# Halving the chunk pairs from the first one on, with the first pair's B and C loaded in blocks: a Mamba-2 scan feeding a PReLU feed-forward layer

## The chip, the cores and the metric

The kernel runs on one core of a Trainium2 chip. The metric is the device time of one execution, in microseconds (us). A core has five engines with queues of their own: TensorE (PE, matrix products), VectorE (DVE), ScalarE (ACT), GpSimd (POOL) and SyncE (SP), which here only issues loads and stores. They meet through semaphores. Sixteen DMA engines move the data.

## The reference

Four batches, eight heads, 768 tokens, head width D = 32, state width N = 16. The first half is a scan over chunks; its output, turned to tokens by features (3072 x 256), goes through a feed-forward layer of width 2048.

```python
for c in range(nc):                          # in chunks
    cum = np.cumsum(log_a, axis=-1)
    L = np.exp(cum[..., :, None] - cum[..., None, :]) * causal
    M = np.einsum('bhin,bhjn->bhij', Cc, Bc) * L
    y_intra = np.einsum('bhij,bhjd->bhid', M, xc)
    y_inter = np.einsum('bhin,bhnd->bhid', Cc, state) * np.exp(cum)[..., None]
    y[:, :, sl] = y_intra + y_inter
    state = decay_full * state + sum_j(B_j x_j decay_from_j)

h = x @ w_in                                 # x: (3072, 256), w_in: (256, 2048)
g = np.maximum(h, 0.0) + alpha * np.minimum(h, 0.0)
return g @ w_out                             # w_out: (2048, 256)
```

x, a, B and C come as float32, the feed-forward weights and alpha in double width; the kernel makes float32 of them.

## The kernel before

The scan works in chunks of Q = 128 tokens, two chunks k = 0, 1 to a pair, twelve pairs `gp`, three to a batch. Four chunks (two pairs) are a group of GT = 512 tokens; the feed-forward layer takes a group at a time.

A pair has these steps. Loads: B and C (`nat`), x (`xt`), the running products of a (`ap`, also called `pf`), and the decays a of each head copied to all partitions (`abc`). B and C are turned so that the state index lies on the partitions (`bc`), either by four transposes on PE (L640, in the opening L807) or by one on VectorE, from loads in blocks of 8 tokens (`turn_bc`, L545). The decays become a triangular matrix for each head by a scan on VectorE (`scan_half`, L532 and L538; in the opening L855 and L908) whose second operand is an identity: `dec`. C is split into even and odd heads (`cz`, L650/L813, ACT) and multiplied by the running product (`cd`, L653/L957, POOL). The gram products C B^T (PE; L713, L702, in the opening L822) are multiplied by `dec` (L724, in the opening L851). `added` (L600, L589, in the opening L831) is what the pair adds to the state: B times its decay to the end (`bn`, L476, POOL) times x. `states` (L613) adds it up on VectorE and POOL masks it (`sm`, L616). Last, the output y is the sum of state products (L768, L750; in the opening L870) and x products (L776, L758; in the opening L878), and ACT copies it to `xT`.

The pairs have two layouts. Pairs 0 to 5 (`gp < HALF`) hold a chunk on all 128 partitions: a head's decay matrix is 128 x 128, so both chunks and eight heads take 2048 columns, of which the upper triangle's blocks are partly zero. Pairs 6 to 11 hold the tokens of chunk k on half k of the partitions, as two sub-blocks j of HQ = 64 tokens. A head then takes only SQ = 192 columns (128 for the first 64 source tokens, 64 for the others), and PE works on tiles of 32 x 64 (gram) or 64 x 32 (the others), the two chunks side by side. The terms that come from the state and cross from one half to the other need copies of `cd` and the masked state moved to the other half of the partitions (`shifted`: L661 on ACT, L663 on POOL).

The stages. `first_two` does pairs 0 and 1 by hand (the opening), and in between the first feed-forward products for the first 256 tokens (`hidden_two`, L1011, called with f = 0 and 2), as soon as the weights of piece 0 are converted. Its loads come from `load_pair(0)`, `load_rows` and `load_a` (decays of a, L133 and L126), `load_pair(1)` and `load_second` (L223). The weights come in 16 pieces of 512 KB (`load_weights`, L249), converted in four steps (`convert_a`, `sign`, `convert_b`, `convert`; L265 to L318). `keep_warm` (L326) issues matmuls on constants whose results aren't used: 8 at the start, 6 before the first gram, 2 before the first x products. Then group 0 is finished with `hidden` (L996, one feature block f on 512 tokens) and `output` (L1034), while pairs 2 and 3, in large pieces, stand in the gaps, and pair 4 begins. From there on five more groups run with fewer products, on sums of blocks of weights and x (L1095 and L1120), and pairs 4 to 11 (`fine`) go in small pieces between them. There `added` of pair gp + 1 stands behind the x products of pair gp, in what is left of the same PSUM tiles (`beside`).

The order on every engine is written out by hand, and each engine works in that order. A DMA issue takes time on the queue that issues it, and SP issues nearly all of them, in the order of the program: in the opening a, al_n, B and C of pair 0 (L188), x (L192), the first two weight pieces, the copy-out of the decays (`rows_out`, L441: z are the decays, pf the products), B, C and x of pair 1, two pieces, pair 2. There are eight DMA semaphores in turn, so an issue also waits for the one eight before it to land.

Of the kernel before, what the change touches and what calls it, by code (L numbers as in the profile page):

```python
# [9 lines left out]
F32 = mybir.dt.float32  # L10
# [12 lines left out]
def kernel(  # L23
# [47 lines left out]
    WARM = 8  # L71
# [8 lines left out]
    HALF = NP // 2  # L80
# [9 lines left out]
    lda = ctx.enter_context(tc.tile_pool(name="lda", bufs=3))  # L90
# [48 lines left out]
    def load_tokens(dst, src, t0):  # L139


        d = dst.rearrange("p j (h w) -> p j h w", h=H)
        for k in range(2):
            for j in range(2):
                t = t0 + k * Q + j * HQ
                nc.sync.dma_start(out=d[HQ * k : HQ * (k + 1), j],
                                  in_=src[:, t : t + HQ, :].rearrange("h p w -> p h w"))

    def load_spread(gp, b, c):

        for w, t in enumerate(loads["p", gp][1] if gp >= HALF else ()):
            rows = scratch["z", b // 2].rearrange("(b h c) t -> b c h t", b=2, h=H)
            for k in range(2):
                nc.sync.dma_start(
                    out=t[HQ * k : HQ * (k + 1), : 4 * SQ].rearrange("p (h t) -> p h t", h=4),
                    in_=rows[b % 2, c + k, 4 * w : 4 * w + 4].unsqueeze(0)
                    .to_broadcast([HQ, 4, SQ]))
        for k, t in enumerate(loads["p", gp][1] if gp < HALF else ()):
            rows = scratch["z", b // 2].rearrange("(b h c) t -> b c h t", b=2, h=H)[b % 2, c + k]
            nc.sync.dma_start(out=t.rearrange("p (h t) -> p h t", h=H),  # L160
                              in_=rows.unsqueeze(0).to_broadcast([P, H, Q]))

    def load_pair(gp, decays=True):


        b, c = divmod(2 * gp, CPB)
        turned = gp > GC
        nat = ldx.tile([P, 3, 2, H * N], F32, name="nat")
        xt = ldx.tile([P, 2, HD], F32, name="xt")

        ap = ldx.tile([P, 2 * Q], F32, name="ap")
        if gp == 0:
            load_a(ap, b, c)
        elif gp >= NB:
            rows = scratch["pf", b // 2].rearrange("(b h c) t -> b h (c t)", b=2, h=H)
            rows = rows[b % 2, :, c * Q : (c + 2) * Q]
            nc.sync.dma_start(out=ap, in_=rows.unsqueeze(1).to_broadcast([H, N, 2 * Q]))
        if gp == 0:
            load_rows(0, nc.scalar)
            nc.sync.dma_start(out=al_n, in_=moe_alpha.rearrange("(k p) -> k p", p=P))  # L180
        abc = []
        later = []
        if gp >= HALF:
            load_tokens(nat[:, 0], B[b], c * Q)
        for k in range(2 if gp < HALF else 0):
            ts = slice((c + k) * Q, (c + k + 1) * Q)
            for i, src in enumerate((B,) if turned else (B, C)):
                nc.sync.dma_start(out=nat[:, i, k].rearrange("p (h n) -> p h n", h=H),  # L188
                                  in_=src[b, :, ts, :].rearrange("h p n -> p h n"))

            def load_x(k=k, ts=ts):
                nc.sync.dma_start(out=xt[:, k].rearrange("p (h d) -> p h d", h=H),  # L192
                                  in_=x[b, :, ts, :].rearrange("h p d -> p h d"))

            if gp < NB:
                later.append(load_x)
            else:
                load_x()
        for load_x in later:
            load_x()  # L200
        if gp == 0:
            loads["a", 1] = prep.tile([P, 2 * Q], F32, name="a1")
            load_a(loads["a", 1], b, c + 2)
        for i, src in enumerate((B, C) if turned else ()):


            for e in range(2):
                first = src[b, e : e + 1, c * Q : (c + 2) * Q, :]
                nc.sync.dma_start(out=nat[:, 1 + e, i],
                                  in_=bass.AP(tensor=first.tensor, offset=first.offset,  # L210
                                              ap=[[2 * S * N, P // 32], [8 * N, 32], [1, 8 * N]]))
        for k in range(2 if gp >= NB else 0):
            abc.append(lda.tile([P, H * Q], F32, name="abc"))
        loads["p", gp] = nat, abc, xt, ap
        if gp >= HALF:
            load_tokens(xt, x[b], c * Q)
        if decays:
            load_spread(gp, b, c)

    def load_second():  # L220

        rows = scratch["pf", 0].rearrange("(b h c) t -> b h (c t)", b=2, h=H)
        nc.sync.dma_start(out=loads["p", 1][3], in_=rows[0, :, 2 * Q : 4 * Q].unsqueeze(1)  # L223
                          .to_broadcast([H, N, 2 * Q]))

    al_n = const.tile([NF, P], F32, name="al_n")
    load_pair(0)
# [95 lines left out]
    def keep_warm(to, n, cols=2 * Q):  # L323

        for i in range(n):
# [6 lines left out]
    ident_h = const.tile([P, H * Q], F32, name="ident_h")  # L332
    nc.vector.tensor_copy(out=ident_h.rearrange("p (h t) -> p h t", h=H),
                          in_=ident.unsqueeze(1).to_broadcast([P, H, Q]))
# [12 lines left out]
    nc.gpsimd.tensor_tensor(out=hmask, in0=hmask, in1=bmask[:, P:], op=ALU.add)  # L347
    zeros = const.tile([P, Q], F32, name="zeros")
    nc.gpsimd.memset(zeros, 0.0)
# [46 lines left out]
    def halve_identity():  # L396

        for s in range(2):
            nc.scalar.copy(
                out=ident_p[0][HQ:].rearrange("p (a s t) -> p s a t", a=2, s=2)[:, s],  # L400
                in_=ident[HQ:, HQ * (1 - s) : HQ * (2 - s)].unsqueeze(1).to_broadcast([HQ, 2, HQ]))

    def rows_swapped():

        prs = prep.tile([RW, Q], F32, name="rpf")
        for h in range(2):
            nc.scalar.copy(out=prs[:, HQ * h : HQ * (h + 1)],
                           in_=held["pr"][:, HQ * (1 - h) : HQ * (2 - h)])
        held["prs"] = prs

    def rows_clamp(i):
        rows = loads.pop(("r", i))
        d0 = prep.tile([RW, SQ], F32, name="r0")
        nc.vector.tensor_scalar(out=d0[:, :Q], in0=rows, scalar1=1e-6, scalar2=1.0,
                                op0=ALU.max, op1=ALU.min)
        if i:
            nc.vector.tensor_scalar(out=d0[:, Q + 1 :], in0=rows[:, HQ + 1 :], scalar1=1e-6,
                                    scalar2=1.0, op0=ALU.max, op1=ALU.min)
        held[i] = d0

# [10 lines left out]
    def rows_out(i):  # L431


        d0 = held.pop(i)[:, : SQ if i else Q]
        rpf = prep.tile([RW, Q], F32, name="rpf")
        nc.vector.tensor_tensor_scan(out=rpf, data0=d0[:, :Q], data1=zeros[:RW], initial=1.0,
# [6 lines left out]
    def rows_turn(i, pr):  # L443
# [8 lines left out]
        if i == 0:  # L452
            nc.scalar.copy(out=t, in_=ps[:, :RW])
# [7 lines left out]
        if i == 0:  # L461
            nc.scalar.copy(out=alpha, in_=ps[:, RW : RW + NF])
# [978 lines left out]
```

## Time and profile before

| what | us |
|---|---|
| median of three runs | 359.79 (358.23 to 360.84) |
| profiled execution, its own time | 359.9 |
| span of its instructions | 358.2 |
| PE busy | 350.5 (98%), 2878 matmuls |
| PE weight loads busy | 288.3 (80%) |
| VectorE busy | 239.9 (67%) |
| ScalarE busy | 173.8 (49%) |
| GpSimd busy | 205.4 (57%) |
| first `hidden` (L996) starts | 28.69 |
| granted TensorE clock | 0.999 |

The page gives the busy time of each engine, then the span in forty slices (about 9 us each; a digit is the busy share in tenths), then the DMA queues and the chain of work that ended last. The other views used are windows (busy time of each engine and count of instructions, clock, DMA share and GB/s between two times), the chain cut to a window, and groups of instructions by line and shape. "SPq" is the issuing queue of SP.

### The profile page before, as it was taken

How to read it: one execution, taken by the hardware profiler on the slowest of the kernel's cores; microseconds unless marked ns; L12 is line 12 of the kernel's file. 1: busy time of each engine (PE TensorE's matmuls, PEld its weight loads, DVE VectorE, ACT ScalarE, POOL GpSimd, SP SyncE). 2: the span in 40 equal slices, each digit the busy share in tenths (PEclk: the TensorE clock that was granted, in tenths of full speed). 3: DMA queues.
4: the chain of work that ended last, by engine and by line, in shares of the span. 5: the costliest groups of instructions: out<-in, count | busy, mean ns of one | idle time of the engine just before them, and what ended most of it. 6: DMA issues, size and time to landing. Idle time of an engine off the chain costs nothing.

```text
span 358.2 us, 7528 instructions
## 1 busy us (share of the span) xinstructions
PE 350.5 (98%) x2878; PEld 288.3 (80%) x2878; DVE 239.9 (67%) x466; ACT 173.8 (49%) x386; POOL 205.4 (57%) x222
## 2 busy tenths in 40 slices
PE   8899999999999999999999999999999999999994
PEld 8676665578788788888888888888888888888883
DVE  6987986998748756857647847757847533654272
ACT  3577666535356346346246345345445343444330
POOL 4876568589939755725655725646726544632521
PEclk9999999999999999999999999999999999999999
DMA  6989999608255403403513413413001002002003
GB/s 110 182 186 303 326 198 258 140 17 176 88 98 118 94 2 76 102 2 88 92 30 85 79 48 79 89 41 73 1 4 29 0 2 31 0 2 30 0 15 77
DMA packets 105453, 30.19 MB, mean 84 GB/s; under 512 B 79864, under 2 KB 101320, under 8 KB 105416
## 3 DMA queue, kind: packets, MB, share of 16 engines
q1 hardware_dynamic: 104488, 29.45, 37.2%
q8 instruction: 23, 0.38, 0.5%
q10 hardware_dynamic: 928, 0.25, 0.3%
q14 instruction: 14, 0.11, 0.1%
HBM read 26.32 MB, written 3.37 MB: 83 GB/s over the span
## 4 chain that ended last, share of the span: by engine, by line
PE 92%; SPq 3%; DMA 1%; DVE 1%; issue 1%; ACT 1%; POOLq 0%
PE bank L1095 34%; PE hp L1120 28%; PE bank L1034 8%; PE hp L996 6%; PE ss L1120 6%; SPq L188 2%; PE hp L1011 2%; PE ss L758 1%; PE ss L702 1%; DMA nat<-in_C_dram 1%; PE ss L750 1%; PE ss L776 1%; PE ss L713 1%; PE ss L589 1%; PE ss L768 0%
## 5 line engine op out<-in xcount | busy, mean ns | idle before, releaser
L1177 POOL TENSOR_TENSOR gt<-gt 128x512 f32<-128x512 f32 x58 | 74.1, 1277 | 21.1 <-DVE gt L1105 16.3
L1095 PE MATMUL bank<-gt,w_out 128*128 128x256 f32 x320 | 83.5, 381 | 0.0
L1095 PEld LDWEIGHTS bank<-gt,w_out 128*128 128x128 f32 x320 | 60.1, 190 | 9.2 <-issue 1.0
L1105 DVE SCALAR_TENSOR_TENSOR gt<-hp,s_mul,gt 128x256 f32<-128x256 f32 x96 | 42.0, 479 | 29.0 <-ACT gt L1103 26.8
L1167 POOL TENSOR_TENSOR gt<-gt 128x512 f32<-128x512 f32 x20 | 25.4, 1269 | 62.6 <-DVE gt L1105 57.2
L1095 PE MATMUL bank<-gt,ws 128*128 128x256 f32 x240 | 59.5, 379 | 0.0
L1103 ACT ACTIVATE gt<-hp,s_alpha 128x256 f32<-128x256 f32 x96 | 40.3, 471 | 34.5 <-PE hp L1120 31.4
L1095 PEld LDWEIGHTS bank<-gt,ws 128*128 128x128 f32 x240 | 45.6, 190 | 6.2
L1120 PE MATMUL hp<-xs,w_in 128*128 128x256 f32 x160 | 41.9, 384 | 0.0
L1120 PE MATMUL hp<-xs,ws 128*128 128x256 f32 x160 | 41.1, 380 | 0.0
L1146 DVE TENSOR_TENSOR hp<-hp,u 128x512 f32<-128x512 f32 x20 | 14.0, 699 | 35.8 <-ACT u L1144 35.8
L1120 PEld LDWEIGHTS hp<-xs,ws 128*128 128x128 f32 x160 | 30.3, 190 | 4.3 <-POOL xs L1075 0.2
L1120 PEld LDWEIGHTS hp<-xs,w_in 128*128 128x128 f32 x160 | 29.7, 190 | 4.5
L1034 PE MATMUL bank<-w_out,gt 128*128 128x256 f32 x128 | 31.0, 384 | 0.0
L1034 PEld LDWEIGHTS bank<-w_out,gt 128*128 128x128 f32 x128 | 23.6, 190 | 6.5 <-issue 3.1
L1120 PE MATMUL ss<-xT,w_in 128*128 128x256 f32 x96 | 24.6, 379 | 0.0
L996 PE MATMUL hp<-xT,w_in 128*128 128x512 f32 x48 | 22.7, 596 | 0.2 <-DVE gt L1023 0.2
L616 POOL TENSOR_TENSOR sm<-state,bmask 128x256 f32<-128x256 f32 (+1 forms) x10 | 6.2, 617 | 29.0 <-DVE state L613 29.0
L532 DVE TENSOR_TENSOR_SCAN dec<-abc,bank 128x192 f32<-128x192 f32 x48 | 22.6, 522 | 0.0
L1135 ACT COPY m<-hp 128x512 f32<-128x512 f32 x8 | 4.7, 586 | 35.7 <-PE hp L1120 35.7
L1144 ACT COPY u<-hp 128x512 f32<-128x512 f32 x20 | 11.7, 585 | 19.4 <-PE hp L1120 19.4
L1105 DVE SCALAR_TENSOR_TENSOR gt<-c,s_mul,gt 128x256 f32<-128x256 f32 x40 | 20.6, 555 | 0.0
(201 smaller groups left out, 609.6 us busy)
## 6 DMA issues: line engine op xcount, KB each, us to landing
abc<-z SPq DMA_DIRECT2D x24, 192.0 KB
raw<-in_moe_w_in_dram SPq DMA_DIRECT2D x8, 512.0 KB
raw<-in_moe_w_out_dram SPq DMA_DIRECT2D x8, 512.0 KB
abc<-z SPq DMA_DIRECT2D x8, 512.0 KB
out_dram<-o_sb SPq DMA_DIRECT2D x32, 64.0 KB
nat<-in_B_dram SPq DMA_DIRECT2D x26, 64.0 KB
nat<-in_C_dram SPq DMA_DIRECT2D x24, 64.0 KB
xt<-in_x_dram SPq DMA_DIRECT2D x12, 128.0 KB
```

Source lines behind the costliest of these rows:

```text
L188: nc.sync.dma_start(out=nat[:, i, k].rearrange("p (h n) -> p h n", h=H), in_=src[b, :, ts, :].rearrange("h p n -> p h n"))
L532: nc.vector.tensor_tensor_scan(out=dv[:, o : o + SQ], data0=abc[k][:, s : s + SQ], data1=ident_p[0][:, :SQ], initial=0.0, op0=ALU.mult, op ...
L996: nc.tensor.matmul(hp, w_in[:, k, f * P : (f + 1) * P], xts[g][:, k], start=(k == 0), stop=(k == KC - 1))
L1034: nc.tensor.matmul(pos[0][t // 2][:, t % 2], gt[:, t * Q : (t + 1) * Q], w_out[:, f], start=(f == 0 and t % 2 == 0), stop=(f == NF - 1), s ...
L1095: nc.tensor.matmul(ms[g][i][:, h], w, blocks[g, z][n][:, p], start=(q == 0 and h == 0), stop=(q == NQ - 1), skip_group_check=True)
L1103: nc.scalar.mul(o[:, p], h[:, p], s_alpha[:, fs[p]])
L1105: nc.vector.scalar_tensor_tensor(out=o[:, p], in0=h[:, p], scalar=s_mul[:, fs[p]], in1=o[:, p], op0=ALU.mult, op1=ALU.max)
L1120: nc.tensor.matmul(to[:, p], w(2 * z + p), b, start=start and p == 0, stop=True, skip_group_check=True)
L1144: nc.scalar.copy(out=u2, in_=A)
L1146: nc.vector.tensor_tensor(out=Y, in0=Y, in1=u2, op=ALU.add)
L1167: nc.gpsimd.tensor_tensor(out=tc_, in0=g22, in1=g12, op=ALU.subtract)
L1177: eng.tensor_tensor(out=o, in0=x0, in1=x1, op=ALU.subtract)
```

## The change

All pairs take the halved layout: the constant HALF and every branch on it go. `rows_turn` turns the decays to the end on PE into the halved order for both halves of the batches; the identity that the scans use is made in the halved form at the start, so `halve_identity` and `rows_swapped` go. The scans and products of pairs 0 to 5 take the narrower shapes. For pairs 2 and 3, `added` no longer has a slot of its own: it stands behind the gram, in the columns that the narrower gram leaves free (`dps_of`).

In the opening, B and C of pair 0 come as blocks of 8 tokens, C's issued by SP and B's by ACT's queue, right after a; VectorE turns them (`turn_blocks`) ahead of its scans. B in token order for `bn` is issued by ACT, x by SP, the second half of it behind the copy-out of the decays. The decays of pair 1 are no longer computed from a second load of a, but read back from the copied-out rows (`load_heads` into `z1`), and its spread on PE has the same form as that of pair 0. al_n is loaded later and turned behind that spread. The first weight piece is still issued ahead of `first_two`, the second now just ahead of pair 1, whose C is loaded ahead of its B. The warm-ups at the start become 6 and the other two groups go. `abc` is one tile for a pair, two buffers deep, in place of two tiles three deep.

The core of the diff, first the loads:

```diff
-    WARM = 8
+    WARM = 6
...
-    HALF = NP // 2
...
-    lda = ctx.enter_context(tc.tile_pool(name="lda", bufs=3))
+    lda = ctx.enter_context(tc.tile_pool(name="lda", bufs=2))
...
+    def load_blocks(nat, i, src, t0, es=(0, 1), eng=nc.sync):
+        for e in es:
+            first = src[e : e + 1, t0 : t0 + 2 * Q, :]
+            eng.dma_start(out=nat[:, 1 + e, i],
+                          in_=bass.AP(tensor=first.tensor, offset=first.offset,
+                                      ap=[[2 * S * N, P // 32], [8 * N, 32], [1, 8 * N]]))
...
+    def load_heads(dst, key, b, c):
+        rows = scratch[key, b // 2].rearrange("(b h c) t -> b h c t", b=2, h=H)
+        rows = rows[b % 2, :, c : c + 2].rearrange("h c t -> h (c t)")
+        nc.sync.dma_start(out=dst, in_=rows.unsqueeze(1).to_broadcast([H, N, dst.shape[1]]))
...
+    def load_first():
+        nat, _, xt, ap = pair_tiles(0)
+        load_a(ap, 0, 0)
+        load_rows(0, nc.scalar)
+        for e in range(2):
+            load_blocks(nat, 1, C[0], 0, (e,))
+            load_blocks(nat, 0, B[0], 0, (e,), nc.scalar)
+        nc.scalar.copy(out=al_n[:, :1], in_=nc.const_aps.tensor(1.0, [NF, 1], F32))
...
-    load_pair(0)
+    load_first()
...
-    load_next(2)
-    rows_clamp(0)
+    load_next()
+    load_tokens(loads["p", 0][2], x[0], 0, (0,))
+    load_tokens(loads["p", 0][0][:, 0], B[0], 0, eng=nc.scalar)
+    rows_clamp(0, nc.gpsimd)
```

The order of the opening in `first_two` after the change (new lines; what they replace is the function shown above):

```diff
+        sp = spread_rows(z0)
+        pr = rows_scan(0)
+        rows_ends(0, nc.gpsimd)
+        rows_product(0)
+        rows_out(0, ("z",))
+        load_tokens(xt0, x[0], 0, (1,))
+        load_heads(z1.rearrange("p k t -> p (k t)"), "z", 0, 2)
+        rows_out(0, ("pf",))
+        nc.sync.dma_start(out=al_n, in_=moe_alpha.rearrange("(k p) -> k p", p=P))
+        load_next()
+        nat1, _, xt1, pf1 = pair_tiles(1)
+        load_chunks(nat1[:, 1], C[0], 2 * Q)
+        load_tokens(nat1[:, 0], B[0], 2 * Q)
+        load_heads(pf1, "pf", 0, 2)
+        load_tokens(xt1, x[0], 2 * Q)
...
+        bc0 = turn_blocks(nat0)
+        rows_turn(0, pr, spare())
...
+        scans(0, sp, (0,))
...
+        scans(0, sp, (1, 2, 3))
+        gram = [ss(), ss(), spare(), spare()]
+        gram_products(bc0, cz, gram)
+        dps = dps_of(gram)
+        added(dps, bn0, xt0)
...
+        sp = spread_rows(z1)
+        nc.tensor.transpose(sp[0][:, 2 * SQ : 2 * SQ + NF], al_n, ident[:NF, :NF])
+        state_products(y, (None, sm0[0][:, 0]), cd0)
+        x_products(y, xt0, dec[0], (False, True), (1, 0))
...
+        scans(1, sp, (0, 1))
+        bc1 = turn_products(nat1, spare())
...
+        scans(1, sp, (2, 3))
...
+        prelus = [hidden_two(0, 0, 0, spare())]
+        gram = [ss(), ss(), bank(0), bank(1)]
+        gram_products(bc1, cz, gram)
+        dps = dps_of(gram)
+        added(dps, bn1, xt1)
```

And in `pair`, for those that are not `fine` (pairs 2 and 3):

```diff
         else:
-            states(added(ss_tile()))
-            c_decayed()
-            spread_c()
-            decays(0)
-            yield
-            decays(1)
+            products_of_c()
+            scan_heads(dec, abc, 0, 2)
+            yield
+            scan_heads(dec, abc, 2, 2)
+            yield
...
+        gram_products(bc, cz, gram)
+        if not fine:
+            dps = dps_of(gram)
+            added(dps, bn, xt, nk)
+            states(dps)
+            move_states()
```

In `gram_products` and `x_products` the loops are those that the halved pairs had before (L702 and L758), now for all pairs.

## The prediction

> **What bounds the kernel now.** I read the page's busy shares first, then the forty slices, then the chain that ended last, and then one window at a time.
>
> ```profile
> PE 350.5 (98%) x2878; PEld 288.3 (80%) x2878; DVE 239.9 (67%) x466; ACT 173.8 (49%) x386; POOL 205.4 (57%) x222
> ...
> PE   8899999999999999999999999999999999999994
> ...
> PE 92%; SPq 3%; DMA 1%; DVE 1%; issue 1%; ACT 1%; POOLq 0%
> ```
>
> TensorE is busy for 98% of 358.2 us and is 92% of the last chain; only the first two slices are below 9. A window over the middle is plainer: no gap in 310 us.
>
> ```profile
> 30.00:340.00 310.00, 310.00 (x2501) 256.01 (x2500) 205.68 (x402) 153.38 (x342) 181.76 (x184) 1.00 0.35 78
> ```
>
> So from 28.69 us, where the first `hidden` (L996) begins, time is won only by taking work off PE, and what the change takes from DVE or adds to ACT and POOL is covered. In the opening PE waits. The chain over 0 to 31 us, in order of time (start, us, what):
>
> ```profile
> 10.11 2.90 SPq L188
> ...
> 13.06 3.57 DMA nat<-in_C_dram
> 16.63 0.04 issue
> 16.67 0.34 PE hp L807
> 17.04 0.59 ACT bc L810
> ...
> 17.77 1.97 PE hp L1011 x8
> ...
> 24.33 0.38 ACT xT L883
> ...
> 24.76 2.01 PE hp L1011 x8
> ```
>
> The SP queue, which issues the loads, ends the wait until 13 us; then the load of pair 1's C, whose transpose starts at 16.67; then PE and its short feeders until the two `hidden_two` of tokens 256 to 511 start at 24.76. The opening is therefore a matter of when loads land, and only then of arithmetic.
>
> **What the skill says.** "TensorE: Matmul & The Clock Gate", section on packing small matmuls, says that matmuls on different 32x32 tiles of the array run at once. The trace agrees. Pairs 2 to 5 do their gram products with 16 matmuls on four row tiles; pairs 6 and 7, already halved, with 32 on eight tiles, skipping half of the upper block. In this order (start:end, us, PE busy and count):
>
> ```profile
> 41.79:42.86 1.07, 1.07 (x17) 1.00 1.09 349
> 63.05:64.12 1.07, 1.07 (x17) 1.00 0.92 124
> 90.36:91.60 1.24, 1.24 (x17) 1.00 0.67 220
> 118.95:120.03 1.08, 1.08 (x18) 1.00 0.66 108
> 146.59:147.43 0.84, 0.84 (x34) 1.00 0.82 140
> 173.73:174.57 0.84, 0.84 (x34) 1.00 0.29 88
> ```
>
> "TensorEngine Tiling (Array Packing)", Key Properties, says that a change of tiling mode drains the engine. The trace shows about 0.09 to 0.10 us more in the large matmul on either side of each small group. Part 1 of the first page says that the array runs at half rate until about 3.4 us of sustained work, and again after an idle window. Here a 128-column warm-up matmul took 213 ns until 5.95 us and 106 to 112 ns after; no idle stretch in before is long enough to show the second half. "DMA: Bandwidth & Descriptors", on why a DMA increments its semaphore by 16, says that the engines used are the largest number up to 16 that divides the outermost dimension. A block load (L209) has 4 outermost; while such loads ran, the DMA share was 0.26, four engines of sixteen (last columns: clock, share, GB/s):
>
> ```profile
> 101.80:104.20 2.40, 2.40 (x12) 2.09 (x12) 1.66 (x4) 2.03 (x6) 0.35 (x1) 1.00 0.26 74
> ```
>
> **The change part by part: the steady stage.** Pairs 6 to 11 are as before. Pairs 2 to 5 take on their layout. Gram: 1.07 + 1.07 + 1.24 + 1.08 = 4.46 us become 4 x 0.84 = 3.36: -1.1. State and x products (with `added` of the next pair from pair 4 on):
>
> ```profile
> 49.96:51.57 1.61, 1.61 (x65) 1.00 0.94 258
> 71.35:72.74 1.39, 1.39 (x50) 1.00 0.04 12
> 97.84:99.56 1.72, 1.72 (x73) 1.00 0.58 159
> 125.41:127.40 1.99, 1.99 (x98) 1.00 0.04 8
> 152.80:154.54 1.74, 1.74 (x114) 1.00 0.04 9
> 179.94:181.61 1.67, 1.67 (x114) 1.00 0.16 45
> ```
>
> The halved ones of pairs 6 and 7 take 1.74 and 1.67. Pair 5 comes down to 1.74 (-0.25) and pair 4 to 1.66 (-0.06). Pairs 2 and 3 lack `added` (0.23 by itself at pair 4), so I take about 1.42 and 1.19: -0.19 and -0.20. Sum -0.7. Then `added` of pairs 2 and 3 leaves its own slots (L600, 0.25 and 0.36) and stands straight behind the gram: it still costs some 0.25 each, but the two pairs of switches, about 0.19 each, go, and the double-size group at 55.60 shrinks: -0.3. In all -2.1 us; the uncertain terms are pairs 2 and 3 and the switches, so -1.7 to -2.5.
>
> Hidden beside it: per pair, DVE loses 8 x (664 - 522) = 1.1 us of scans and 4 x (680 - 550) = 0.5 of products. ACT gains two copies of C's product at 297 ns, POOL two of the state at 287. The decays of a pair shrink from 1 MB to 0.79 MB, and two whole-pair buffers replace three half-pair ones. If that cover failed PE would show gaps; the same pieces show none in pairs 6 to 11.
>
> **The change part by part: the opening.** Removed on PE: transposes of pair 0 (0.66), the second spread (L511, 32 by 288 ns, overlapped), and warm-ups of 6 and 2. On DVE: scans of 1206 ns over 512 columns become 384 columns; from 522 for 192 and 664 for 256 I estimate 0.95, and eight save 2.0 us. Added on DVE: one transpose of blocks (L545's row, 1113 ns) in front of those scans.
>
> Timing by hand. (1) B's and C's first blocks are four DMAs of 128 packets on four engines, which `ap` uses too; the similar 512 packets at 101.8 took 4.1 us. They land near 7.0 (5.5 if the queues drain as `ap` did at 3.6, 7.8 if the two issuing queues interleave badly). The transpose then ends near 8.1, and DVE, in order, holds its scans behind it, although their PE input is there from about 6. (2) DVE finishes pair 0's scans near 12 and its last product at 13.4; its x products end near 15.5, where before they ended at 15.78. (3) On SP some 17 issues stand before the last load of pair 1, at 0.41 to 0.65 us each. Eight may be outstanding, so three of them also wait for a landing: second half of x for C's block, the copy-out of the decays for B's, the next for weight piece 0 (near 8.9). The last of pair 1's B is issued near 16, where C was issued at 14.5 before, and lands near 17.6; the last of x near 21.0. (4) From there: transposes to 18.0, `hidden_two` 1.9, gram 0.84, `added` waits for x until 21.3, states 0.6, the mask on POOL 0.73, moving it on ACT 0.3, products 1.35 and 0.84 beside it, two copies 0.75, both needed before L906. It starts near 25.9 against 24.76: +1.1 (1.0 to 1.4). (5) If blocks land at 5.5 and no issue waits, DVE bounds instead and L906 starts at 22.3 to 23.5: -1.3 to -2.5. I take the middle of (4) and (5), a wash, and keep both ends.
>
> The warm-ups taken away leave PE idle for 2 to 3.3 us about 13 us in. Bounds: nothing, if the small groups still count as work; at most the 1.95 us of a `hidden_two` run at half rate plus as much of the next, 1.9 to 3.4. I take nothing, as each stretch is below 3.4.
>
> **Sum.** 359.9 (profiled) - 2.1 + 0 = 357.8; the median 359.79 stands 0.1 lower: 357.7. A change of 1%, 3.6 us, is about what a measurement of this kernel can tell.
>
> **Rivals.** A, likeliest: the steady gain, the opening a wash: 357.7, own range 356.3 to 359.1. For it: the two ends of the opening lie about equally far on both sides.
>
> B: pair 1's loads aren't stalled and the blocks land early: -2.1 - 2.5 = 355.2. For it: the chain shows 2.90 + 1.46 us of SP waiting at L188, and removing loads from SP onto ACT's queue shortens just that; DVE has 2.0 us less. Against it: 17 issues at 0.6 are 10 us whatever lands.
>
> C, slower: the SP queue reaches pair 1's x late, PE idles meanwhile and comes to the dense stage at half rate. Price: opening +1.4 (up to +4.3 if one issue waits 2.90 for a weight piece, as at 10.11 before), +1.9 for the cold clock, -2.1: 361.0 to 363.9, say 362.5. It decides once PE idles for more than 3.4 us in one stretch before `hidden_two`. For it: without the warm-ups only small matmuls run between 8 and 17 us. Against: before, the weight pieces pass through the same ring and the stage starts on time.
>
> D: the change does not do in the stage what it says: the gain on PE is eaten by gaps, since `added`, states, mask and the moves of pairs 2 and 3 now all follow the gram. From the gram to the state products there are 7.1 us (42.86 to 49.96) for about 0.25 + 0.6 + 0.73 + 0.57, so I hold it unlikely: 359.8.
>
> **How the numbers follow.** A 0.40, B 0.38, C 0.17, D 0.05. Faster by over 1% (below 356.2): nearly all of B, 0.36, and A's tail, 0.05: 0.41. Slower by over 1% (above 363.4): the upper part of C, 0.08. Within: 0.51. Range: B reaches to 354.0 with the opening at -2.5, the stage at -2.5 and 0.8 for the DVE time not accounted for; C is taken in to 361.6. That leaves out some 0.05 below and 0.12 above.
>
> **What would show it.** Right: gram groups of 0.84 in all of pairs 2 to 5, L600's slots gone, PE without a gap between the first `hidden` and 340 us, DVE near 231 us (239.9, less 4 x 1.6 in the pairs, less 2.0 of scans and 0.6 of products in the opening, plus 1.1). For the opening, the start of the dense stage (28.69 before) tells A (within 1), B (2 or more earlier) and C (2 or more later). The chain would name SP and the x or B load of pair 1 in A, DVE in B. Matmuls of 128 columns at about 213 ns after 8 us would show C's clock. Wrong: small groups of pairs 2 to 5 above 1.0 us, or PE gaps in the stage.

## The result, and the profile after

The changed kernel takes 368.66 us (368.17 to 369.12) against 359.37 for the kernel before: ratio 1.0256, 95% interval 1.0214 to 1.0298. The forecast was 357.7 with a range of 354.0 to 361.6. The profiled execution has a span of 367.1 us, 8.9 more than before. Its page, in the same order:

```profile
PE 349.5 (95%) x3235; PEld 287.7 (78%) x3235; DVE 231.2 (63%) x469; ACT 175.6 (48%) x402; POOL 209.0 (57%) x231
...
PE   5568999999999999999999999999999999999996
...
PE 78%; DMA 6%; DVE 5%; POOL 4%; ACT 2%; SPq 2%; issue 1%; POOLq 0%; DVEq 0%; ACTq 0%
```

PE does 1.0 us less work (349.5 against 350.5) and VectorE 8.7 us less, near the 231 us that the prediction gave. The time is lost in waits: the first four slices fell from 8, 8, 9, 9 to 5, 5, 6, 8, and the chain, 92% PE before, is 78% now. Four points on PE divide the loss (us, the last column worked out):

| | before | after | |
|---|---|---|---|
| first `hidden_two` starts | 17.77 | 23.12 | +5.35 |
| from there to the third (tokens 256 on) | 6.99 | 8.91 | +1.92 |
| first `hidden` (L996, now L891) starts | 28.69 | 35.96 | +7.27 |
| from there to the last products (the stage) | 324.35 | 327.44 | +3.09 |
| from there to the end of the span | 5.2 | 3.7 | -1.5 |

The last products of before, of after and of g3_stage (an experiment below), each from its own trace:

```profile
353.04 0.44 PE L1220 MATMUL turned<-ident,c 128*128 128x128 f32 x2 [0.28 <-DVE c L1246]
...
363.40 0.44 PE L1115 MATMUL turned<-ident,c 128*128 128x128 f32 x2 [0.27 <-DVE c L1141]
...
360.18 0.44 PE L1120 MATMUL turned<-ident,c 128*128 128x128 f32 x2 [0.27 <-DVE c L1146]
```

So the opening lost 7.3 us, where a wash was forecast, and the stage lost 3.1, where 2.1 were to be gained. The last row is no effect of the change. There the outputs only have to be copied out and land: fifteen of the eighteen profiled executions of this document take 3.6 to 3.9 us for it, and three (those of before, d2_sum and h2_order) 5.0 to 5.2. Whoever reads the stage up to the end of the span takes this difference for a gain.

PE's waits in the opening (engine and operation that waited, what it waited for: us in all, times, longest) were six small ones before; L1011 waiting 0.8 for `bc` was the longest but for the start. After:

```profile
PE ss L540 <- POOL cz L728: 4.4, 1, 4.4
PE bank L469 <- DVE dec L546: 1.6, 1, 1.6
PE hp L502 <- issue: 1.5, 1, 1.5
PE hp L502 <- DMA nat<-in_B_dram: 1.4, 1, 1.4
...
```

The gram (L540) and `added` (L519, 0.9 us) of pair 0, the spread (L469) and the transposes (L502) of pair 1 all wait for something. The chain over the first 45 us:

```profile
2.26 4.65 DMA nat<-in_C_dram
...
7.00 4.76 DMA z<-r
...
18.57 3.81 DMA nat<-in_B_dram
...
23.33 2.95 PE hp L906 x8
```

It goes through two landings up to 11.8: the block load of C (SP issues the copy-out of the decays at 7.0, after it), and that copy-out, which the read-back of pair 1's decays (L176) needs. SP's own waits up to 24 us show a third landing beside them, and a longer one, that of weight piece 0:

```profile
SPq L145 <- DMA raw<-in_moe_w_in_dram: 2.7, 1, 2.7
SPq L427 <- DMA nat<-in_C_dram: 1.5, 1, 1.5
...
SPq L176 <- DMA z<-r: 0.4, 1, 0.4
```

From 7.4 to 10.1 SP stands at the second half of x, which it issues until 11.4; only 0.4 us are left to the copy-out alone. Then fifteen issues follow each other up to 22.9, pair 1's last B among them at 18.57, and it lands at 22.39. The `hidden_two` behind it ran partly at half rate (2.95 us against 1.97).

In the stage, the gram groups of pairs 2 to 5, which the prediction put at 0.84 (start:end, elapsed, PE busy and count):

```profile
48.61:50.42 1.81, 1.47 (x33) 1.00 1.02 377
70.53:72.62 2.09, 1.48 (x34) 1.00 0.53 50
...
```

Pairs 2 and 3 stop in the middle; pairs 4 and 5 take 0.98 and 1.17. PE has gaps of 1.86 us in all between 49 and 90 us, where before had none, all but 0.06 of it put down to gt on VectorE (L895), which frees the PSUM tile that comes next. Among the waits of all engines from 36 to 130 us, the longest that before does not have is no PE wait:

```profile
ACT moved_c L635 <- POOL cd L632: 7.0, 4, 3.3
```

The next such wait is VectorE's for the loaded decays, 3.3 us in two stops.

### The profile page after: what moved, and what is told of

The parts are those of the page before. It is cut to its first block, busy times and chain, and to the rows that moved or that the text cites. A ratio compares the mean times of both kernels' runs of the same rounds, so it can differ in the third digit from the quotient of the medians.

```text
span 367.1 us, 8302 instructions
## 1 busy us (share of the span) xinstructions
PE 349.5 (95%) x3235; PEld 287.7 (78%) x3235; DVE 231.2 (63%) x469; ACT 175.6 (48%) x402; POOL 209.0 (57%) x231
## 4 chain that ended last, share of the span: by engine, by line
PE 78%; DMA 6%; DVE 5%; POOL 4%; ACT 2%; SPq 2%; issue 1%; POOLq 0%; DVEq 0%; ACTq 0%
PE bank L990 33%; PE hp L1015 28%; PE ss L1015 5%; DMA raw<-in_moe_w_in_dram 3%; PE bank L929 2%; PE hp L906 2%; PE ss L560 2%; PE ss L540 2%; DMA z<-r 1%; DMA nat<-in_C_dram 1%; PE ss L685 1%; DVE gt L895 1%; POOL w_out L308 1%; DMA nat<-in_B_dram 1%; PE hp L891 1%
## 5 line engine op out<-in xcount | busy, mean ns | idle before, releaser
L484 DVE TENSOR_TENSOR_SCAN dec<-abc,bank 128x192 f32<-128x192 f32 x80 | 37.8, 526 | 3.3 <-DMA abc<-z 3.3
L525 POOL TENSOR_TENSOR sm<-state,bmask 128x256 f32<-128x256 f32 (+1 forms) x13 | 8.1, 620 | 30.7 <-DVE state L598 27.7
L891 PE MATMUL hp<-xT,w_in 128*128 128x512 f32 x48 | 22.7, 596 | 0.6 <-DVE gt L895 0.4
L1015 PE MATMUL hp<-xT,ws 128*128 128x256 f32 x80 | 20.5, 379 | 0.0
```

What stands on the lines that cost most here:

```text
L484: nc.vector.tensor_tensor_scan(out=dec[:, h], data0=abc[:, h * SQ : (h + 1) * SQ], data1=ident_p[0][:, :SQ], initial=0.0, op0=ALU.mult, op ...
L525: nc.gpsimd.tensor_tensor(out=sm.rearrange("p k (g m) -> p k g m", g=2), in0=new[:, ks].unsqueeze(2).to_broadcast([P, n, 2, 2 * D]), in1=h ...
L891: nc.tensor.matmul(hp, w_in[:, k, f * P : (f + 1) * P], xts[g][:, k], start=(k == 0), stop=(k == KC - 1))
L1015: nc.tensor.matmul(to[:, p], w(2 * z + p), b, start=start and p == 0, stop=True, skip_group_check=True)
```

## The experiments

All were compared with the kernel before on the same chip. "Start" is where the first `hidden` begins in the one profiled execution, "stage" the time from there to the last products, "rest" from there to the end of the span, with the landing of the outputs in it.

| kernel | ratio (95%) | start | stage | rest |
|---|---|---|---|---|
| before | 1 | 28.69 | 324.4 | 329.5 |
| after | 1.0256 (1.0214 to 1.0298) | 35.96 | 327.4 | 331.1 |
| b1_stage | 1.0100 (1.0071 to 1.0129) | 29.1 | 329.2 | 333.0 |
| c1_later | 1.0050 (1.0033 to 1.0067) | 28.9 | 325.6 | 329.2 |
| c4_abc | 1.0204 (1.0171 to 1.0238) | 29.0 | 332.9 | 336.6 |
| c6_xlater | 1.0035 (1.0021 to 1.0049) | 28.8 | 326.2 | 330.0 |
| g3_stage | 1.0203 (1.0170 to 1.0237) | 36.5 | 323.7 | 327.4 |
| a1_warm | 1.0259 (1.0215 to 1.0304) | 35.8 | 329.3 | 333.2 |
| a2_z1 | 1.0252 (1.0212 to 1.0291) | 36.5 | 327.6 | 331.4 |
| a3_first | 1.0261 (1.0219 to 1.0303) | 37.8 | 325.8 | 329.6 |
| d1_noblock | 1.0214 (1.0187 to 1.0242) | 34.6 | 327.6 | 331.2 |
| d2_sum | 1.0176 (1.0144 to 1.0207) | 34.1 | 327.1 | 332.2 |
| e1_order | 1.0209 (1.0194 to 1.0224) | 36.8 | 325.9 | 329.5 |
| e2_tail | 1.0218 (1.0191 to 1.0246) | 33.5 | 326.1 | 329.7 |
| g1_waits | 1.0200 (1.0166 to 1.0234) | 33.5 | 327.3 | 331.0 |
| g2_all | 1.0139 (1.0097 to 1.0182) | 32.5 | 328.5 | 332.1 |
| h1_best | 1.0127 (1.0094 to 1.0160) | 33.8 | 324.0 | 327.7 |
| h2_order | 1.0049 (1.0027 to 1.0070) | 29.9 | 327.6 | 332.6 |

A start is good to some 2.4 us only: e1_order and e2_tail have the same opening up to the first `hidden_two` and begin it at 22.24 and 19.83 in their profiled executions. These are single executions and need not be typical. Those of e1_order and g2_all are the longest of their runs, 2.2 and 2.8 us above the median, and that of e2_tail is the shortest.

**The stage by itself.** b1_stage takes the opening of before and the halved pairs from 2 on.

```diff
-        load_first(), first_two() of after
+        load_pair(0), load_pair(1), first_two() of before (128 partitions)
...
     identity_bank()
+    halve_identity()
+    rows_turn(0, held['pr'], ss_tile())      # pairs 2 to 5: halved order
     bns[2] = pair_loads(2)
```

> The kernel after, but with the opening of before: its loads, their order, its warm-ups, pairs 0 and 1 on 128 partitions. Only pairs 2 to 5 are halved; the decays to the end of batches 0 and 1 are turned once more (eight small matmuls, about 0.7 us with the switches). If the opening alone made the change slow: the first L891 starts within 0.6 us of 28.7, no gap over 0.1 us in the stage up to 90 us, and the time is 359.4 - 2.1 + 0.7 = 358.0. If the halved pairs themselves make the waits that the trace after shows between 49 and 90 us (gaps of 1.85 us, gram groups of 1.81 and 2.08 us): these show here too, and the time is about 361.

It is slower than before by 1.0%. The second answer came true, and beyond its number: the opening is back at 29.1, and the gaps are there (3.25 us), with gram groups of 1.95 and 2.11. The stage takes 329.2 us against 324.4. So the halved pairs lose time by themselves, even where the opening is that of before. ScalarE, 38 to 43 us (start, us, operation, idle before it), then GpSimd at the same time:

```profile
38.27 0.91 ACT L677 ACTIVATE cz<-bc,par 128x256 f32<-128x256 f32 x2
40.53 0.62 ACT L681 COPY moved_c<-cd 64x128 f32<-64x128 f32 x2 [1.35 <-POOL cd L678]
41.57 0.67 ACT L265 ACTIVATE wt<-raw 128x512 f32<-128x512 f32 x1 [0.42 <-DMA raw<-in_moe_w_in_dram]
```

```profile
38.55 1.27 POOL L318 TENSOR_TENSOR w_out<-wr,wg 128x512 uint32<-128x512 uint32 x1 [0.88 <-DVE wr L296]
39.77 0.73 POOL L678 TENSOR_TENSOR cd<-bc,ap 128x256 f32<-128x256 f32 x1
42.40 0.82 POOL L267 TENSOR_SCALAR wt<-wt 128x512 f32<-128x512 f32 x1 [1.90 <-ACT wt L265]
```

The two copies take 0.6 us. But `cd`, which they copy, stands on GpSimd behind a weight conversion that waits for VectorE, so ScalarE stands still for 1.35 us, the next weight's first step comes later, GpSimd waits 1.90 for that, and VectorE and PE are next. Over 28 to 92 us it is 5.1 us of such waits in three stops.

c1_later moves only these copies (pairs 2 and 3), behind the gram:

```diff
         def products_of_c():
...
-            for k, (to, frm) in enumerate(others):
-                nc.scalar.copy(out=moved_c[to], in_=cd[frm, k])
+            if fine:
+                move_c()
...
             states(dps)
             move_states()
+            move_c()
```

> b1_stage (opening of before, pairs 2 to 5 halved) with one edit: for pairs 2 and 3 the copies of C's product to the other half stand on ScalarE behind the gram, no longer ahead of it. In b1_stage ScalarE waited 5.1 us in three stops at these copies for GpSimd's product, with weight conversions and gt behind them. If this wait in the queue makes PE's gaps in the stage: they shrink to under 1 us in all and the time falls from 1.010 to 1.000 or less of before (3.5 us). If late loads of the decays or weights make them: the ratio stays above 1.006.

The wait is gone from ScalarE's list, the gaps fall to 0.75 us, the stage to 325.6, and the ratio to 1.005: half of the loss, between the two answers. g3_stage makes the same edit in the kernel after.

> The kernel after with one edit: for pairs 2 and 3 the copies of C's product stand behind the gram on ScalarE. If this copy makes the stage's waits in the kernel after as it does in b1_stage: ScalarE's 7.0 us at moved_c goes, the gram groups of pairs 2 and 3 shrink from 1.81 and 2.08 to under 1.2 us, and the ratio falls from 1.0256 to about 1.021. If weights that come late with the opening make them: 1.024 or more.

Without a gap from the first `hidden` to 350 us, and with the gram groups of pairs 2 and 3 at their full rate, the stage takes 323.7 us, 3.8 less than after and 0.7 less than before. (Up to the end of the span it is 2.1 less than before, but 1.5 of that are the outputs, which landed late in the profiled execution of before.) First a window, then the four gram groups, then the state and x products of pairs 2 to 5:

```profile
36.52:350.00 313.48, 313.48 (x2762) 260.49 (x2763) 205.17 (x410) 157.49 (x355) 185.33 (x191) 1.00 0.37 75
```

```profile
49.18:50.02 0.84, 0.84 (x35) 1.00 1.04 379
69.80:70.64 0.84, 0.84 (x34) 1.00 0.52 61
97.25:98.23 0.98, 0.98 (x33) 1.00 0.90 159
126.03:127.21 1.18, 1.18 (x34) 1.00 0.41 82
```

```profile
57.45:58.88 1.43, 1.43 (x97) 1.00 0.87 138
78.10:79.50 1.40, 1.40 (x81) 1.00 1.11 223
104.47:106.15 1.68, 1.68 (x113) 1.00 0.57 158
132.58:134.54 1.96, 1.96 (x129) 1.00 0.51 35
```

ScalarE waits 2.3 us at moved_c in place of 7.0 (pairs 4 and up still have it where it was), while VectorE still waits 2.0 for the decays, so that wait did not stop PE here. The ratio fell by 0.005, which is 1.9 us of the 3.8 that the two profiled executions show; the intervals, from different comparisons, still overlap, so the case rests on ratio and trace together, and on b1_stage against c1_later, whose intervals do not overlap.

Why c1_later keeps only part is not settled: its stage is 1.9 us longer than that of g3_stage. One candidate is weights that come late. ScalarE waits there 5.4 us in three stops for weight pieces, against 1.8 in before. In before, pieces 4 and 5 are issued at 25.98 and 26.65, in b1_stage at 27.99 and 28.66, since pair 2 has ten loads of B, C and x in place of six. How dear that is, c4_abc shows, meant as a test of another wait:

```diff
         load_next(2)
-        load_pair(2, False)
-        load_next(2)
-        load_spread(2, *divmod(4, CPB))
+        load_pair(2)                # x, then the decays, then the pieces
+        load_next(2)
```

> b1_stage with one edit: the loads of pair 2's decays are issued right behind its x, ahead of two weight pieces. If VectorE's wait for them at 39.2 us (1.36 us) starts the stage's gaps: it goes, and the ratio falls from 1.010 by 0.004 or more. If ScalarE's queue is the cause: under 0.002, or slower as weight pieces come 1.2 us later.

A miss on both: the decays (0.79 MB) ahead of the pieces cost 1% more, and PE stops for 4.1 us at 36.6, for the converted piece, which, issued 0.9 us later, lands behind them (ScalarE waits 6.6 us for it).

c6_xlater and h2_order go the other way, x of pair 2 later; h1_best as well.

```diff
-        load_pair(2, False)
+        load_pair(2, False, False)          # without x
         load_next(2)
         load_spread(2, *divmod(4, CPB))
+        load_tokens(loads["p", 2][2], x[0], 4 * Q)   # c6; h1, h2: after convert_next, ahead of the loop
```

> c1_later with one edit: the four loads of pair 2's x are issued behind the next two weight pieces and the pair's decays; x is needed only behind the gram now. If the remaining loss of c1_later (0.005, with ScalarE waiting 5.4 us in three stops for weight pieces) comes from pieces issued 2 us later than in before: the pieces are issued near 25.3 in place of 28.0, PE's gap of 0.55 us at 38.2 goes, and the ratio falls from 1.005 to between 0.994 and 0.999. If it comes from work added on the engines: it stays at 1.004 or above.

> c1_later (opening of before, pairs 2 to 5 halved, copies behind the gram) with the second turn of the decays in PE's wait ahead of the first hidden_two instead of in the stage (0.7 us with the switches), and pair 2's x issued behind eleven weight pieces in place of four. If the halved stage is worth the 2.1 us that g3_stage shows for it (327.4 us from the first L891 to the end, 329.5 before) and only late weights hide it in c1_later: the stage takes 327.5 to 328, starts near 28.7, and the ratio is 0.993 to 0.996. If weights still come late, as the decays of pair 2 stand ahead of them in the queues: gaps of 0.5 to 1.5 us remain and the ratio is 0.998 to 1.004.

> h1_best with the second turn of the decays back in the stage (in h1_best its PSUM tile held the second hidden_two for 2.9 us and the stage began at 33.8). If the early start and the halved stage can be had together once weights are issued ahead of pair 2's x: starts at 28.9, no gap over 0.3 us, 328.4 us to the end, ratio 0.996 to 1.000. If the weights that the early start waits for are the limit: gaps of 0.5 to 1.5 us as in c6_xlater, and 1.002 to 1.005.

c6_xlater gained 0.0015 at most (the intervals overlap). It issued pieces 4 and 5 at 24.33 and 24.95, earlier than before does, and ScalarE still waits 6.2 us for pieces, so their place in the queue is not the cause by itself. In h1_best the stage takes 324.0 without a gap, but it began at 33.8. Its second `hidden_two` waited 2.9 us, by the profile for GpSimd's g_add, and then took 2.89 us in place of 1.99. h1_best also moves the second turn of the decays into the opening; h2_order takes only this back, and the wait is gone and the ratio 0.008 lower, with intervals apart. So the turn made that wait; that it did so by keeping the PSUM tile is my reading. In h2_order the x loads came so late that in the profiled execution `added` waited 2.4 us for them, and the ratio is that of c1_later. This execution is one of its two longest (364.24, median 361.62). So the stage shows a gain only where it starts late and loads have had time, and that gain is small: 0.7 us in g3_stage, 0.3 in h1_best. With the early start I found no order of loads that gives both, and no version that beats the kernel before. The stage gain that the expectations of h1_best and h2_order build on, 2.1 us, is the one that has the late outputs of before in it.

**The opening.** Three edits to the kernel after, each alone.

```diff
 a1_warm
-    WARM = 6
+    WARM = 8
+        keep_warm(gram[0], 8)                # ahead of the first gram
+        keep_warm(tp1, 5)                    # ahead of pair 1's transposes
 a2_z1
-        load_heads(z1..., "z", 0, 2)
+        load_a(loads["a", 1], 0, 2)          # in load_first; z1 made by GpSimd
 a3_first
+        load_chunks(nat1[:, 1], C[0], 2 * Q)
+        load_tokens(nat1[:, 0], B[0], 2 * Q)
         load_heads(z1..., "z", 0, 2)
         rows_out(0, ("pf",))
...
         load_next()
-        load_chunks(nat1[:, 1], C[0], 2 * Q)
-        load_tokens(nat1[:, 0], B[0], 2 * Q)
```

> The kernel after, with warm-up matmuls: 8 at the start, 8 of 256 columns ahead of the first gram, 5 of 256 columns ahead of pair 1's transposes. If the cold clock carries the loss: the first eight of L906 take 1.9 us in place of 2.95, and the time falls by 1 to 3 us. If loads carry it: L906's first eight still start near 23.3, and the time falls by 1.05 us at most.

> The kernel after, with pair 1's decays computed from a second load of a (as in before), so SP no longer waits at 11.8 us for the copied-out rows to land. If that read-back is what holds the queue: everything behind it on SP is 1.5 to 1.7 us earlier, pair 1's last B is issued near 17.6, the first L891 starts near 34.3 and the time falls by 1.7. If the queue is held by the sum of its issues or by weight piece 0 instead: less than 0.7.

> The kernel after, with the six issues of pair 1's C and B moved ahead of the read-back of the decays, the products, al_n and the second weight piece. If the place in SP's queue sets when pair 1 begins: B's last issue ends near 15 in place of 19.2, its transposes start 2 to 3 us earlier (then held by the spread, which waits for the read-back, now near 17.5), and the time falls by 1.5 to 3. If the time is set by something else behind it (ACT's order, the cold clock): under 0.5.

None changed the time by more than its interval, 0.004 or 1.5 us either way. a1_warm did what it should to the clock: the first `hidden_two` took 1.89 us, but began at 23.5, and the third at 31.9, against 32.0 without the edit. So no gain came of the full rate there; a part of 1 us would not show in the ratio. The mean clock of an execution does not settle this either: that of g3_stage's profiled execution is 1.000, and its first `hidden_two` took 3.62 us. In a2_z1 SP ran into landings a little later (2.07, 1.54 and 1.59 us at three issues of pair 1). In a3_first pair 1's last B is issued 3 us earlier, but the read-back of its decays later, and PE waits 5.95 us at the spread. In each trace another wait stood where the first had gone.

d1_noblock takes the blocks out.

```diff
-        for e in range(2):
-            load_blocks(nat, 1, C[0], 0, (e,))
-            load_blocks(nat, 0, B[0], 0, (e,), nc.scalar)
+        load_tokens(nat[:, 0], B[0], 0, eng=nc.scalar)
+        load_chunks(nat[:, 1], C[0], 0)
...
-        bc0 = turn_blocks(nat0)
         rows_turn(0, pr, spare())
+        bc0 = turn_products(nat0, spare())
```

> The kernel after with one edit: pair 0's B and C without blocks. B comes once, in token order, issued by ScalarE's queue where the blocks were, C in two chunks, and PE turns them. If the four block loads (four DMA engines, B loaded twice, ScalarE's queue held until 8.7 us) delay pair 0: its gram starts near 8.5 in place of 10.43, added no longer waits for bn at 12.9, x products end 2 to 3 us before 19.2, and the time falls by 1 to 2 us, more if SP's waits for landings go with it. If SP's later issues alone set the start of the stage: less than 0.7.

1.5 us won by the ratios (1.0256 to 1.0214), but the intervals overlap, and the first `hidden_two`, 2.3 us earlier, moved no more than two executions of one opening differ. So this gain is not shown. The gram did not start earlier (11.8), against the expectation; what came earlier was the rest. The landings in the traces do show what the blocks did to the loads behind them. With blocks, the four loads land one behind the other at 4.8, 5.8, 6.9 and 8.0, 1.1 us each, on four DMA engines. Weight piece 0, issued behind them, was done on twelve engines by 7.5 us and on the four others at 9.9 to 10.1, and SP's issue of the second half of x, eight issues later, waits for it from 7.4 to 10.1. Without blocks piece 0 lands on all engines between 7.8 and 8.6. B in token order, whose last load ScalarE's queue issued only at 8.1, was late too, hence L519's wait for bn.

d2_sum puts everything together; e1_order is d2_sum without the added warm-ups; e2_tail moves the third piece's conversion behind the copies to xT; g1_waits changes d2_sum; g2_all adds to g1_waits the stage edits of c1_later and c6_xlater.

```diff
 g1_waits
+        nc.sync.dma_start(out=al_n, ...)     # fifth issue on SP, in d2_sum the eighteenth
-        spread_c(bc0, 1, nc.gpsimd)
+        spread_c(bc0, 1, nc.scalar)
-            nc.scalar.copy(out=o[to], in_=t[frm])
+            nc.gpsimd.tensor_copy(out=o[to], in_=t[frm])   # for the state
```

> d1_noblock with all of a1 to a3 together: pair 1's decays from a second load of a, pair 1's C and B ahead of the products, al_n and the second weight piece, and warm-ups (8, then 4 and 3 of 256 columns). If the opening's 7.3 us are several waits lying side by side, each hidden behind the others when only one goes: the first L891 starts near 30 (28.7 to 31.5) in place of 35.96 and the time falls by 5 to 6 us, to about 363. If one cause outside these edits holds it (the number of issues of pair 1's token-order loads): it starts near 34 and the time falls by 2 at most.

> d2_sum without its warm-ups (6 at the start, as after). In d2_sum the 8 of 256 columns ran at half rate for 3.6 us and held pair 0's gram until 13.1, though its C was ready at 11.5. If pair 0's chain feeds the start: gram near 11.5, hidden_two near 19.7 in place of 21.2, and the ratio falls from 1.0176 by 0.002 to 0.005. If the cold clock is worth more than that: hidden_two takes 2.5 to 3 us again and the ratio rises.

> e1_order with the conversion of the third weight piece (wt and wg on ScalarE, 1.35 us, and what follows on GpSimd) behind pair 1's two copies to xT. If ScalarE's order is what holds the last part of the opening (from the second hidden_two to the third, 4.6 us after, 3.66 before): the third starts 1.0 to 1.4 us earlier than in e1_order, relative to the second, and the time falls by up to that. If the products of pair 1 hold it (GpSimd's mask and multiply): under 0.4, and the piece comes later for the stage, so no gain or a loss.

> d2_sum with the small waits of pair 0 taken out: al_n loaded second on SP as in before, both halves of C's split on ScalarE, the copies of the masked state on GpSimd right behind the mask, and warm-ups cut to 8, 2 and 1. If the rest of the opening (34.1 us in d2_sum against 28.7 in before) is such waits, one behind the other in the queues: the first L891 starts near 31.5 and the ratio falls from 1.0176 to 1.010 or 1.012. If it is the later landing of pair 1's token-order loads: it starts within 1 us of 34 and the ratio stays above 1.015.

> g1_waits with the two edits to the stage as well (pair 2's and 3's copies of C's product behind the gram, pair 2's x behind the weight pieces and decays). If the losses of opening and stage add up: 0.005 to 0.007 below g1_waits. If the stage's waits come from the late opening alone: no difference.

Together they win 0.008 in d2_sum, about 2.9 us: more than the blocks alone, half of what the first answer gave. e1_order lies 0.003 above it, with overlapping intervals, though the warm-ups hold the gram for 3.6 us. In its profiled execution the two `hidden_two` ahead of the first `hidden` took 5.39 us together, in place of 3.72 in d2_sum: there half rate did cost time on the path. e2_tail changed nothing, so ScalarE's conversion isn't what holds the end of the opening. g1_waits (al_n is its fifth issue on SP, not the second) is a miss: its state copies on GpSimd waited in that queue (PE stood 2.2 us at L754). g2_all is 0.006 below g1_waits, as expected if opening and stage add up; the intervals overlap, so it supports this and no more. Its profiled execution shows a rival to the copies as well: with the copies moved, PE still stops for 1.46 us in the gram of pair 2, waiting for gt, after ScalarE stood 3.44 us at a weight piece ahead of gt. So a late weight can stop PE at the same place as the copies did.

What stays open: about 4 us of the opening even in g2_all (32.5 against 28.7), and more in the others. In the six kernels from d1_noblock on, the first `hidden_two` begins between 19.8 and 22.2 (17.8 before), and from there to the third it takes 8.2 to 9.8 us (7.0 before). In the traces the second part is the halved pair's longer chain: in d2_sum PE waits 0.6 us for the moved state and 0.3 for a product ahead of the last products, and for two copies to xT where before one was hidden behind the other half. For the first part the landings of pair 1's B (2.0 us of waits in d2_sum) and al_n (1.4) are named. No run separated the layout of pairs 0 and 1 from their loads.

## Why the prediction was wrong

**Right.** What bounds the stage, the gram groups of 0.84 in pairs 2 and 3 once nothing stops PE, and VectorE's relief (231.2; the terms given for "near 231" add up to 232.0), which was worth nothing.

**The size of the stage's gain was wrong.** The sum gave 2.1 us, 1.7 at the least. With the stops gone PE gains 0.7. That 327.4 against 329.5, up to the end of the span, gives just 2.1 is luck. Term by term, before against g3_stage:

| term | forecast | measured |
|---|---|---|
| gram groups of pairs 2 to 5 | -1.1 | 4.46 to 3.84: -0.6 |
| state and x products of pairs 2 to 5 | -0.7 | 6.71 to 6.47: -0.2 |
| `added` of pairs 2 and 3 | -0.3 with the switches | 0.61 to 0.73: +0.1 |
| turn of the decays | 0 | 0.17 to 0.49: +0.3 |
| what is left, in the large matmuls | | -0.3 |

The gram groups of pairs 4 and 5 took 0.98 and 1.18, not 0.84. The products of pairs 3 and 5 took 1.40 and 1.96, not 1.19 and 1.74.

**The step that failed in the stage** is "Hidden beside it": ScalarE's two copies at 297 ns were priced by their length, and the sentence that pairs 6 to 11 show no gap was taken as cover. Those pairs stand where no weights are converted any more. Where they are, the price was the wait in front of the copies and what stood behind them: 3.8 us between the profiled executions of after and g3_stage, 1.9 by their ratios. Rival D named gaps as its sign but looked for them on the path from gram to state products. It was ScalarE's order.

**The step that failed in the opening** is (3), and with it (4). Pair 1's last B was put at an issue near 16 and a landing near 17.6; it was 18.57 to 19.2 and 22.4: +4.8 of the 6.1 us by which the third `hidden_two` (32.0) missed 25.9. Four terms were mis-sized: piece 0's landing (8.9, measured 10.1; four engines had the blocks ahead of it, and it landed by 8.6 without them), +1.2; the read-back of the decays, which waits for its own copy-out until 11.8 and was not in the list of waits, +0.4; two issues of pair 1's C and B that took 1.45 and 1.12 where their neighbours take 0.6, +1.4; and a landing of 1.6 us after issue, measured 3.2. Of the remaining 1.3, 1.0 is `hidden_two` at half rate, for which the prediction took nothing, since it held each idle stretch of PE to be below 3.4 us. The one before pair 0's gram was 4.35, and ahead of this `hidden_two` stood two of 1.52 and 1.40 with one transpose between them. But a1_warm, which ran it at the full rate, came to the third no more than 0.2 us earlier, so what that 1.0 was worth stays open. (1) was off by 1.2: the transpose began at 8.24, not 7.0.

**Rivals.** C had the mechanisms: SP late, PE idle over 3.4 us (4.35 at 6.08), half rate. Its price ended at 363.9 since it counted one stalled issue and kept the stage's gain. The middle between an early and a late opening was no estimate: all that was known against the early one (17 issues at 0.6 us) stood in the text.

Of the pages of the Trainium skill, "TensorE: Matmul & The Clock Gate", Part 1, is borne out: PE is idle from 6.08 to 10.43, and the gram's groups of eight then start at 10.43, 10.91 and 11.34, where those of pair 6 follow each other at 156.96, 157.23 and 157.44. (The later half rate, at 23.33, came without a single idle stretch of 3.4 us.) So is "DMA: Bandwidth & Descriptors", on why a DMA increments its semaphore by 16, on the number of engines: weight piece 0, issued behind the four block loads, fell behind on four engines of sixteen. What followed from it here is that piece 0 was complete only at 10.1, and SP's issue of x waited 2.7 us for it. One reading is not borne out: the warm-ups of before start 213 ns apart up to 4.16 us and 111 ns apart from 7.23, and none stands between, so they don't show a change at 5.95.

## What to carry to other kernels

Price a copy by what it waits for and what stands behind it in its engine's order, not by its length alone; a place where the same copy is harmless shows nothing for a place where its producer's queue is full. A load on few DMA engines can make later loads late as well: here a load over all sixteen was complete only when the four that had the blocks were done, and through the ring of outstanding loads the issuing queue stood still too. When a path is held by several landings, taking one away may show nothing (a1_warm, a2_z1, a3_first, each within its interval; together with the blocks' removal they won 2.9 us): count the waits side by side before giving a gain to one of them. And when two profiles are compared, end the stretch at the last product, not at the end of the span: here a late landing of the outputs in one of the two made a gain of 0.7 us look like 2.1, the number that was expected.

## What the runs showed of the hardware

In the kernel after, weight piece 0 was complete on twelve of sixteen engines 2.5 us before the last four (7.5 and 9.9 to 10.1). A 32 KB load of 64-byte pieces landed 3.2 us after its issue ended, with a 512 KB piece among the loads ahead of it. Issues on SP that stood for nothing took 0.60 to 0.64 us for each of these 32 or 64 KB loads in token order, so that ten of them are 6 us of queue. From the last products to the end of the span, the same code took 3.6 to 3.9 us in fifteen profiled executions and 5.0 to 5.2 in three. And a mean clock of 1.000 does not exclude half rate in the opening: g3_stage's profiled execution has it, with 3.62 us for a `hidden_two` that took 1.97 in before.
